# Five small moves in the order of work: P1's copy, the fills beside attention and routing, the keys' sums, a query transpose, and the weighing of kept results

## The chip, the cores and the metric

The kernel runs on one core of a Trainium2 chip. The metric is the time of one execution on the device, in microseconds (us); the profile shows one execution of the same program. Five engines run their own instruction queues in order and meet through semaphores: TensorE (PE), VectorE (DVE), ScalarE (ACT), GpSimd (POOL) and SyncE (SP), which here only issues DMA transfers.

## The reference

All arithmetic is in float32. The first half is an attention with a polynomial sketch in place of a softmax, over 4 batches, 4 heads, 1088 tokens and a head size of 32:

```python
def phi(x):                       # r = 8, so 64 features
    a = np.einsum('rd,bhsd->bhsr', S1, x)
    b = np.einsum('rd,bhsd->bhsr', S2, x)
    return np.einsum('bhsi,bhsj->bhsij', a, b).reshape(*x.shape[:-1], r * r)
kv  = np.einsum('bhsf,bhsd->bhfd', phi(k), v)
z   = np.sum(phi(k), axis=2)
num = np.einsum('bhsf,bhfd->bhsd', phi(q), kv)
den = np.einsum('bhsf,bhf->bhs', phi(q), z)[..., None] + 1e-06
attn = num / den
```

Its output, as 4352 tokens of 128 values, is the input x of the second half, eight experts with Sinkhorn weights:

```python
P = np.exp(x @ w_gate - (x @ w_gate).max())
for _ in range(8):
    P /= P.sum(1, keepdims=True) + 1e-09
    P /= P.sum(0, keepdims=True) + 1e-09
    P *= N / E
for e in range(E):                # w1[e]: 128 x 1024, w2[e]: 1024 x 128
    out += P[:, e:e + 1] * (np.maximum(x @ w1[e], 0.0) @ w2[e])
```

## The kernel before

**Two streams in one order.** The experts' work is by far the larger part. It is a generator, `steps` (from L1124), that yields after each small step: one `first` product (x times w1, L929, followed by the relu on ScalarE, L933) and the `second` products (h times w2, L1114) that are due then, `LAG` = 8 steps after the block that they belong to began. `fill(n)` (L1189) draws steps from it until n shares are used up; a step of 480 columns is one share, so that a step of 256 columns is 0.53 and one of 416 is 0.87. Attention and routing are written around it: they issue some instructions, and then `fill` or a `yield` puts expert work behind them on the queues. A larger number at such a place means that more expert work stands ahead of what comes next. The order on TensorE and DVE is kept as written (`manual_schedule`); ScalarE, GpSimd and SyncE follow a scheduler once the start is over, except where `keep_in_program_order` stands.

**Experts ahead of routing.** Before the routing weights are known, the kernel computes some expert results without weights and keeps them in SBUF (`kept`): all tokens for expert 0, and tokens 0 to 511 and 512 to 1279 for expert 1. These are the groups ahead of `PLAIN`. The other groups scale x by the weight first (`prepare_x`, which writes `xe` on GpSimd), and `weigh_kept` multiplies the kept results by their weights on GpSimd, from `pb`, a broadcast load of the weights. It does so once in each weighted group, and what it gives is added to the sums later.

**Products by sums.** The second products use schemes with fewer multiplications (seven products for 2 x 2 blocks, twenty for 3 x 4 blocks). DVE makes the sums of hidden blocks that they need (L946 for seven, L993 and L1013 for twenty), and the products accumulate in four PSUM banks `s`, which the next group uses again. When a bank of a group is complete, `part` takes it apart. In `part_of_seven` bank 0 holds P1; ScalarE copies its two halves crosswise to `z`, DVE adds P1 itself to z (L756), and P1 stays in the bank (`own["p1"] = s`) until bank 1 has been copied to `m`: then `add_now(y1[lower], own["p1"][lower], m[lower])` is queued on DVE, behind whatever was recorded before.

**Attention.** Batch 0 has a path of its own at the start. For batches 1 to 3, `attention(b)` sums over the keys (`keys_sums`, L352, into a PSUM bank), copies that to `kvs` (`keys_kept`, L368 on DVE and L370 on ScalarE), multiplies the query factors in three parts (`times`, L468, where `rb` arrives by DMA), forms the numerators (`tops`, L477 and L481), divides (`over`), and sends the result through DRAM to `xT` (`take_over`). Between these the next batch's keys and queries are prepared, among them `transpose_q(3)` and `keys_products`.

**Routing.** `routing` computes logits (L511), and then eight rounds: DVE makes row sums, reciprocals and column sums `cs`; after a yield of 4.5 shares TensorE adds `cs` over the partitions (L621). The weights go to DRAM (`pT`), from where `xe` and `pb` are loaded.

**The end.** `last_part` puts together the last group's output. For k == 2 it ends with a transpose and store of y2 (`put`), and one add that y1's last sum needs.

Of the kernel before, what the change touches and what calls it, by code (L numbers as in the profile page):

```python
# [50 lines left out]
def kernel(  # L51
# [307 lines left out]
    def keys_kept(b):  # L359
        pv = sums_of.pop(b)  # L360
        for s in range(2):
            sl = slice(64 * s, 64 * (s + 1))
            if b:
                x, y = kvs[b % 2][sl, :, s, :], pv[sl].rearrange("p i c d -> p i (c d)")[:, :, 0:D + 1]
            else:
                x, y = kvz[sl, :, :, s, :], pv[sl].rearrange("p i c d -> p c i d")
            if s and b:
                nc.vector.tensor_copy(x, y)  # L368
            else:
                nc.scalar.copy(x, y)  # L370

    chunks = ((0, 512), (512, 800), (800, S))

# [148 lines left out]
    def attention(b):  # L522


        follows = b + 1 < B
        keys_sums(b)
        times(b, 0)
        yield 1.4
        keys_kept(b)
        times(b, 1)  # L530
        tops(b, 0)
        if b == 1:
            transpose_q(2)
        yield 1.4
        times(b, 2)
        over(b, 0)
        tops(b, 1)
        if b == 1:
            queries_ab(2)
            repeat_a(2)  # L540
        if follows:
            repeat_b(b + 1)
        yield 1.4
        over(b, 1)
        if b + 1 == B:
            take_over(b, 0, 192, nc.gpsimd)
        yield 1.4
        tops(b, 2)
        if follows:
            transpose_k(b + 1)  # L550
        if b + 2 < B:
            load_k(b + 2)
            load_v(b + 2)
        yield 1.4
        over(b, 2)
        if b + 1 < B:
            take_over(b, 0, W9, nc.gpsimd)
        else:
            take_over(b, 192, W9, nc.sync)
        if follows:  # L560
            yield 0.7
            keys_ab(b + 1)
            yield 0.7
            keys_products(b + 1, 0)
            if b == 1:
                transpose_q(3)
            yield 1.4
            keys_products(b + 1, 1)
            if b == 1:
                queries_ab(3)  # L570
                repeat_a(3)
            yield 1.4
            keys_products(b + 1, 2)
            yield 1.4
# [11 lines left out]
    def routing():  # L586

        yield 5
        for c in range(len(chunks)):
            logits(c)  # L590
        yield 1
        for c in range(len(chunks)):
            logits_turned()
        lg = lgp[:, :, 0:E]
        mx = sk.tile([P, 1], F32, tag="mx", name="mx")
        nc.vector.tensor_reduce(out=mx, in_=lg, axis=AX.XY, op=Alu.max)
        yield 3
        pm = bank()[:, 0:P]
        for s in range(2):
            nc.tensor.matmul(pm[64 * s:64 * (s + 1)], mx.to_broadcast([P, 64]), ident, start=True, stop=True,  # L600
                             tile_position=(0, 64 * s))
        nc.vector.reduce_max(mx, pm, axis=AX.X)
        nc.vector.tensor_scalar(mx, mx, -1.0, 64 * math.log(2.0), op0=Alu.mult, op1=Alu.add)
        pw = p2s[0]
        nc.scalar.activation(out=pw[:, :, 0:E], in_=lg, func=Act.Exp, bias=mx[:, 0:1])

        step = 1.5 * 2.0 ** (23 - 149 + 64)
        nc.vector.tensor_scalar(pw[:, :, 0:E], pw[:, :, 0:E], step, step, op0=Alu.add, op1=Alu.subtract)
        for it in range(ITERS):
            rs = sk.tile([P, SA], F32, tag="rs", name="rs")  # L610
            nc.vector.reduce_sum(rs, pw, axis=AX.X)
            nc.vector.reciprocal(rs, rs)
            p1 = p1s[it % 2]
            nc.vector.scalar_tensor_tensor(p1[:, 0:SA], rs.unsqueeze(2).to_broadcast([P, SA, E]), UP,
                                           pw[:, :, 0:E], op0=Alu.mult, op1=Alu.mult)
            cs = sk.tile([P, E], F32, tag="cs", name="cs")
            nc.vector.reduce_sum(cs, p1.rearrange("p g e -> p e g"), axis=AX.X)
            yield 4.5
            pc = bank()[:, 0:E]
            for s in range(2):  # L620
                nc.tensor.matmul(pc[64 * s:64 * (s + 1)], ones[:, 0:64], cs, start=True, stop=True,  # L621
                                 tile_position=(0, 64 * s))
            cr = sk.tile([P, E], F32, tag="cr", name="cr")
            nc.vector.reciprocal(cr, pc)
            last = it == ITERS - 1
            pw = lgp if last else p2s[(it + 1) % 2]
            nc.vector.scalar_tensor_tensor(pw[:, :, 0:E], cr.unsqueeze(1).to_broadcast([P, SA, E]),
                                           float(N) / E * (1.0 if last else UP), p1[:, 0:SA],
                                           op0=Alu.mult, op1=Alu.mult)

        nc.vector.transpose(out=lgT.rearrange("p a s -> p (a s)"), in_=lgp.rearrange("p a e -> p (a e)"))
        for b in (1, 0, 2, 3):
            nc.sync.dma_start(out=pT[:, b * S:(b + 1) * S],
                                                  in_=lgT[32 * b:32 * b + E].rearrange("p a s -> p (a s)"))
# [71 lines left out]

    first_weighted = next(j for j, (g, e) in enumerate(items) if g == PLAIN)

    def weigh_kept(g):

        lo, n, t, es, _ = groups[g]
        ys = []
        for e in range(es[0]):
            ys.append(kept[e][:, lo:lo + n * t])
            weigh(ys[e], ys[e], weights_of(e, lo, n * t, "pb"))
        for y in ys[1:]:
            tc.keep_in_program_order(nc.gpsimd.tensor_tensor(ys[0], ys[0], y, op=Alu.add))
        if t == 2:
            k1, k2 = ys[0][upper, 0:n], ys[0][upper, n:2 * n]
            tc.keep_in_program_order(nc.gpsimd.tensor_tensor(k1, k1, k2, op=Alu.subtract))  # L720
# [26 lines left out]
    def part_of_seven(g, k):  # L747

        lo, n, _, es, _ = groups[g]
        s = sums[g][k]  # L750

        def add(out, a, b):
            at_leisure(lambda: nc.vector.tensor_tensor(out, a, b, op=Alu.add))

        def add_now(out, a, b):
            soon.append(lambda: nc.vector.tensor_tensor(out, a, b, op=Alu.add))  # L756

        own = parts.setdefault(g, {})
        y1, y2 = (kept[es[0]][:, lo + t * n:lo + (t + 1) * n] for t in range(2))
        if k == 0:  # L760
            z = own["z"] = room("z", n)
            nc.scalar.copy(z[lower], s[upper])
            nc.scalar.copy(z[upper], s[lower])
            add_now(z, s, z)
            own["p1"] = s
        elif k == 1:
            m = own["m"] = room("m", n)
            nc.scalar.copy(m, s)
            add_now(y1[lower], own["p1"][lower], m[lower])
        elif k == 2:  # L770
            w, f = own["w"], own["f"] = room("w", n), room("f", n)
            nc.scalar.copy(w[lower], s[lower])
            nc.scalar.copy(f[lower], s[upper])
            nc.scalar.copy(f[upper], s[upper])
        else:
            r = room("r", n)
            nc.scalar.copy(r[upper], s[lower])
            own["r"] = r
            own["p7"] = s
        own[k] = True  # L780
        z, w, f, m = (own.get(x) for x in "zwfm")
        if all(own.get(x) for x in (0, 2, 3)) and "v" not in own:
            own["v"] = True
            add_now(w[upper], own["p7"][upper], own["r"][upper])
            add(z, z, w)
            add(y2, z, f)
        if all(own.get(x) for x in range(4)):
            add(y1[upper], z[upper], m[upper])
# [9 lines left out]
    def last_part(g, k):  # L798
# [5 lines left out]
        def add(out, a, b):  # L804
            nc.vector.tensor_tensor(out, a, b, op=Alu.add)
# [10 lines left out]
        elif k == 2:  # L816
            nc.scalar.copy(r[lower], s2[upper])
            nc.scalar.copy(x[lower], s0[lower])
            add(y2[upper], z[upper], s2[upper])
            add(y2[lower], s2[lower], r[lower])  # L820
            put(y2, lo + n, n, (nc.sync, nc.scalar))
            add(x[upper], x[upper], s2[upper])
        else:
            add(y1, s1, x)
            put(y1, lo, n, (nc.sync, nc.scalar))
# [298 lines left out]
    def steps():  # L1124

        todo, sums_at, t = {}, {}, 0
        for k in range(len(blocks) + 5):
# [5 lines left out]
            if k < len(blocks):  # L1133
# [13 lines left out]
                    w = w1, w2, sums_of_two(items[j + 1][1], w2)  # L1147
                    loaded_w.update({i: w for i in loaded_w if items[i][1] == items[j + 1][1]})
                if q == 0:
                    if weighted and e == es[3 if tiles == 3 else 2]:  # L1150
                        weigh_kept(g)
                if k == len(blocks) - HELD:
                    kept_to_sums(g)
                m, step, sums_ = (four if tiles == 3 else two)(k)
# [63 lines left out]
    with tc.manual_schedule(engines={engines.DVE, engines.PE}):  # L1218
# [1 line left out]
            multiply(1, i)  # L1220
        transpose_k(1)
        load_k(2)
        fill(0.75)
        fractions(1, 1)
        fractions(1, 0)
        fill(0.75)
# [61 lines left out]
```

## Time and profile before

| what | value |
|---|---|
| time, median of 3 runs (lowest to highest) | 932.78 us (928.51 to 933.78) |
| span of the profiled execution, granted TensorE clock | 927.0 us, 0.999 |
| DVE busy, 100 to 125, 125 to 150, 150 to 175 us | 18.01, 22.59, 22.03 of 25 |
| ScalarE busy in the same stretches | 12.03, 12.79, 13.09 of 25 |
| GpSimd's wait for `pb` to land | 47.2 us in 5 waits |
| `kept` weighed by GpSimd near 400 us, two multiplies | 4.12 us |

The profile page gives each engine's busy time, its idle time with what ended it, and the chain of work that ended last. An idle stretch of an engine that isn't on that chain costs nothing. The first numerators follow some 34 us after the start, the logits come at 105.6 us, the weights go to DRAM at 174.8, and the first product of a weighted group starts at 191.9; from there to the end the work is regular.

### The profile page before, as it was taken

How to read it: one execution, taken by the hardware profiler on the slowest of the kernel's cores; microseconds unless marked ns; L12 is line 12 of the kernel's file. 1: busy time of each engine (PE TensorE's matmuls, PEld its weight loads, DVE VectorE, ACT ScalarE, POOL GpSimd, SP SyncE). 2: the span in 40 equal slices, each digit the busy share in tenths (PEclk: the TensorE clock that was granted, in tenths of full speed). 3: DMA queues.
4: the chain of work that ended last, by engine and by line, in shares of the span. 5: the costliest groups of instructions: out<-in, count | busy, mean ns of one | idle time of the engine just before them, and what ended most of it. 6: DMA issues, size and time to landing. Idle time of an engine off the chain costs nothing.

```text
span 927.0 us, 18876 instructions
## 1 busy us (share of the span) xinstructions
PE 914.0 (99%) x7466; PEld 552.6 (60%) x7466; DVE 673.4 (73%) x1140; ACT 412.6 (45%) x888; POOL 211.3 (23%) x220
## 2 busy tenths in 40 slices
PE   9999999999999999999999999999999999999997
PEld 6777444456666666655555555555555555556886
DVE  7544688797879697685876666965657977768665
ACT  3333455554444454434544444544445444445443
POOL 3031300093546402030120101101010224320220
PEclk9999999999999999999999999999999999999999
DMA  9994100213354434453444434363434365553640
GB/s 252 310 273 153 52 1 1 76 56 109 125 166 159 154 130 144 133 186 110 148 126 155 147 121 136 114 189 125 148 109 155 101 200 183 172 181 92 173 153 12
DMA packets 91303, 128.13 MB, mean 138 GB/s; under 512 B 25392, under 2 KB 69504, under 8 KB 86480
## 3 DMA queue, kind: packets, MB, share of 16 engines
q1 hardware_dynamic: 88384, 121.42, 41.7%
q0 software_dynamic: 1600, 5.36, 2.0%
q8 instruction: 58, 0.95, 0.4%
q10 hardware_dynamic: 1232, 0.16, 0.1%
q14 instruction: 29, 0.24, 0.1%
HBM read 107.88 MB, written 19.05 MB: 137 GB/s over the span
## 4 chain that ended last, share of the span: by engine, by line
PE 95%; DVE 3%; ACT 1%; issue 1%; POOL 0%; DVEq 0%; ACTq 0%; POOLq 0%
PE a L929 49%; PE s L1114 42%; PE a L352 1%; PE a L477 1%; PE a L114 1%; DVE hb L993 1%; PE a L319 0%; DVE pqg L993 0%; PE s L384 0%; PE a L441 0%; ACT hb L933 0%; PE s L407 0%; DVE kept L756 0%; PE a L511 0%; PE a L390 0%
## 5 line engine op out<-in xcount | busy, mean ns | idle before, releaser
L929 PE MATMUL a<-xe,w 128*64 128x256 f32 (+1 forms) x2560 | 519.5, 470 | 0.0
L933 ACT ACTIVATE hb<-a 128x256 f32<-128x256 f32 (+4 forms) x408 | 195.3, 480 | 257.8 <-PE a L929 231.7
L933 ACT ACTIVATE hx<-a 128x256 f32<-128x256 f32 (+1 forms) x360 | 167.4, 465 | 214.2 <-PE a L929 193.8
L929 PEld LDWEIGHTS a<-xe,w 128*64 128x64 f32 x2560 | 208.2, 137 | 77.2 <-issue 1.4
L1114 PE MATMUL s<-hb,ws 128*64 128x256 f32 (+2 forms) x1248 | 214.1, 395 | 0.6 <-DVE hb L993 0.6
L993 DVE TENSOR_TENSOR hx<-hx 128x512 f32<-128x512 f32 (+1 forms) x204 | 157.6, 783 | 68.2 <-ACT hx L933 62.7
L1114 PE MATMUL s<-hx,ws 128*64 128x256 f32 x1280 | 206.0, 379 | 0.7 <-DVE kept L756 0.7
L993 DVE TENSOR_TENSOR hb<-hb 128x512 f32<-128x512 f32 (+1 forms) x204 | 134.5, 670 | 92.2 <-ACT hb L933 88.0
L693 POOL TENSOR_TENSOR xe<-xT,xe 128x768 f32<-128x768 f32 (+2 forms) x41 | 83.3, 2032 | 499.3 <-DMA xe<-pT 485.0
L1114 PEld LDWEIGHTS s<-hx,ws 128*64 128x64 f32 x1280 | 106.7, 137 | 97.4 <-issue 74.0
L1114 PEld LDWEIGHTS s<-hb,ws 128*64 128x64 f32 x1248 | 101.9, 137 | 103.4 <-issue 80.0
L1114 PE MATMUL s<-hb,w 128*64 128x256 f32 (+3 forms) x616 | 116.5, 406 | 2.7 <-DVE kept L756 2.7
L929 PE MATMUL a<-xT,w 128*64 128x416 f32 (+3 forms) x512 | 117.3, 462 | 0.1
L1114 PEld LDWEIGHTS s<-hb,w 128*64 128x64 f32 x616 | 54.0, 137 | 35.6 <-issue 15.2
L1114 PE MATMUL s<-hx,w 128*64 128x256 f32 x384 | 68.5, 379 | 0.0
L929 PEld LDWEIGHTS a<-xT,w 128*64 128x64 f32 x512 | 47.0, 137 | 28.4 <-issue 21.5
L242 POOL TENSOR_TENSOR ws<-w 128x256 f32<-128x256 f32 (+1 forms) x70 | 60.1, 894 | 14.7 <-DMA w<-in_moe_w_dram 10.6
L946 DVE TENSOR_TENSOR hb<-hb 128x416 f32<-128x416 f32 (+3 forms) x60 | 46.4, 774 | 18.7 <-ACT hb L933 10.4
L946 DVE TENSOR_TENSOR hx<-hx 128x256 f32<-128x256 f32 (+1 forms) x65 | 39.1, 607 | 24.4 <-ACT hx L933 23.2
L993 DVE TENSOR_TENSOR pqg<-hb 128x512 f32<-128x512 f32 x68 | 44.5, 696 | 0.0
L1114 PEld LDWEIGHTS s<-hx,w 128*64 128x64 f32 x384 | 34.4, 137 | 10.3
L993 DVE TENSOR_TENSOR pqg<-hx 128x512 f32<-128x512 f32 x68 | 37.4, 591 | 0.0
(183 smaller groups left out, 466.6 us busy)
## 6 DMA issues: line engine op xcount, KB each, us to landing
w<-in_moe_w_dram SPq DMA_DIRECT2D x82, 512.0 KB, 5.3
ws<-ws SPq DMA_DIRECT2D x34, 1024.0 KB, 5.0
xe<-pT SPq DMA_DIRECT2D x34, 384.0 KB, 4.1
ws<-ws SPq DMA_DIRECT2D x12, 512.0 KB, 4.7
ph<-qa SPq DMA_DIRECT2D x12, 288.0 KB, 5.4
rb<-qb SPq DMA_DIRECT2D x3, 1152.0 KB, 7.9
pb<-pT SPq DMA_DIRECT2D x6, 384.0 KB, 7.5
kx<-in_k_dram SPq DMA_DIRECT2D x4, 544.0 KB, 4.9
```

The lines of the kernel that those rows point to most:

```text
L114: nc.tensor.matmul(warm[:, 0:P], ones, ones, start=True, stop=True)
L242: tc.keep_in_program_order(nc.gpsimd.tensor_tensor(ws[:, c:c + len(ns)], blocks(x), blocks(y), op=Alu.subtract if off else Alu.add))
L352: nc.tensor.matmul(pv[64 * s:64 * (s + 1), i], kp[0:n, H * t + h].rearrange("p i j -> p (i j)"), vx[0:n, slots[h], t, :], start=(t == 0 an ...
L477: nc.tensor.matmul(pn[64 * s:64 * (s + 1), t, 2 * i:2 * i + 2].rearrange("p h d -> p (h d)"), ph[:, i, s, 64 * t:64 * (t + 1)], kvs[b % 2] ...
L693: tc.keep_in_program_order(nc.gpsimd.tensor_tensor(out, x, pb, op=Alu.mult))
L929: nc.tensor.matmul(ph[sl], loaded_w[j][0][:, P * f + H2 * s:P * f + H2 * (s + 1)], sources[j][:, lo:hi], start=True, stop=True, tile_posit ...
L933: nc.scalar.activation(out=out, in_=ph, func=Act.Relu)
L946: nc.vector.tensor_tensor(out, a, b, op=Alu.subtract)
L993: nc.vector.tensor_tensor(out if not isinstance(out, tuple) else places(*out), places(*a), places(*b) if isinstance(b, tuple) else b, op=A ...
L1114: nc.tensor.matmul(sums[g][i][H2 * s:H2 * (s + 1), n * place:n * (place + 1)], w, x, start=c == 1, stop=c == per, tile_position=(0, H2 * s))
```

## The change

The edits are:

- `keys_kept`: both halves of the keys' sums are copied by ScalarE; one was DVE's.
- `attention`: more expert work between the keys' sums and the first numerators (2.2 shares for batch 1, 1.7 for batches 2 and 3, from 1.4), so that TensorE has work while the numerators' inputs get ready. `transpose_q(3)` comes ahead of the first keys' product.
- At the start, `fill(1.25)` in place of 0.75 ahead of batch 0's second fractions.
- `routing`: 4.25 shares per round in place of 4.5.
- `weigh_kept`: one multiply for each expert of the group, from its second on, in place of all in one go at the fourth (third in the last group).
- `part_of_seven`: the lower half of P1 is copied out of PSUM by ScalarE, to a buffer `x`, and the later add reads the copy.
- `last_part`: y1's add is put ahead of y2's transpose and store.

```diff
@@ -364,10 +364,7 @@
                 x, y = kvs[b % 2][sl, :, s, :], pv[sl].rearrange("p i c d -> p i (c d)")[:, :, 0:D + 1]
             else:
                 x, y = kvz[sl, :, :, s, :], pv[sl].rearrange("p i c d -> p c i d")
-            if s and b:
-                nc.vector.tensor_copy(x, y)
-            else:
-                nc.scalar.copy(x, y)
+            nc.scalar.copy(x, y)
 
     chunks = ((0, 512), (512, 800), (800, S))
 
@@ -525,7 +522,7 @@
         follows = b + 1 < B
         keys_sums(b)
         times(b, 0)
-        yield 1.4
+        yield 2.2 if b == 1 else 1.7
         keys_kept(b)
         times(b, 1)
         tops(b, 0)
@@ -561,9 +558,9 @@
             yield 0.7
             keys_ab(b + 1)
             yield 0.7
-            keys_products(b + 1, 0)
             if b == 1:
                 transpose_q(3)
+            keys_products(b + 1, 0)
             yield 1.4
             keys_products(b + 1, 1)
             if b == 1:
@@ -615,7 +612,7 @@
                                            pw[:, :, 0:E], op0=Alu.mult, op1=Alu.mult)
             cs = sk.tile([P, E], F32, tag="cs", name="cs")
             nc.vector.reduce_sum(cs, p1.rearrange("p g e -> p e g"), axis=AX.X)
-            yield 4.5
+            yield 4.25
             pc = bank()[:, 0:E]
             for s in range(2):
                 nc.tensor.matmul(pc[64 * s:64 * (s + 1)], ones[:, 0:64], cs, start=True, stop=True,
@@ -706,13 +703,13 @@
 
     first_weighted = next(j for j, (g, e) in enumerate(items) if g == PLAIN)
 
-    def weigh_kept(g):
+    def weigh_kept(g, i):
 
         lo, n, t, es, _ = groups[g]
-        ys = []
-        for e in range(es[0]):
-            ys.append(kept[e][:, lo:lo + n * t])
-            weigh(ys[e], ys[e], weights_of(e, lo, n * t, "pb"))
+        ys = [kept[e][:, lo:lo + n * t] for e in range(es[0])]
+        if i < len(ys):
+            weigh(ys[i], ys[i], weights_of(i, lo, n * t, "pb"))
+            return
         for y in ys[1:]:
             tc.keep_in_program_order(nc.gpsimd.tensor_tensor(ys[0], ys[0], y, op=Alu.add))
         if t == 2:
@@ -761,8 +758,9 @@
             z = own["z"] = room("z", n)
             nc.scalar.copy(z[lower], s[upper])
             nc.scalar.copy(z[upper], s[lower])
+            own["p1"] = room("x", n)
+            nc.scalar.copy(own["p1"][lower], s[lower])
             add_now(z, s, z)
-            own["p1"] = s
         elif k == 1:
             m = own["m"] = room("m", n)
             nc.scalar.copy(m, s)
@@ -818,8 +816,8 @@
             nc.scalar.copy(x[lower], s0[lower])
             add(y2[upper], z[upper], s2[upper])
             add(y2[lower], s2[lower], r[lower])
+            add(x[upper], x[upper], s2[upper])
             put(y2, lo + n, n, (nc.sync, nc.scalar))
-            add(x[upper], x[upper], s2[upper])
         else:
             add(y1, s1, x)
             put(y1, lo, n, (nc.sync, nc.scalar))
@@ -1147,8 +1145,8 @@
                     w = w1, w2, sums_of_two(items[j + 1][1], w2)
                     loaded_w.update({i: w for i in loaded_w if items[i][1] == items[j + 1][1]})
                 if q == 0:
-                    if weighted and e == es[3 if tiles == 3 else 2]:
-                        weigh_kept(g)
+                    if weighted and 1 <= es.index(e) <= es[0] + 1:
+                        weigh_kept(g, es.index(e) - 1)
                 if k == len(blocks) - HELD:
                     kept_to_sums(g)
                 m, step, sums_ = (four if tiles == 3 else two)(k)
@@ -1220,7 +1218,7 @@
             multiply(1, i)
         transpose_k(1)
         load_k(2)
-        fill(0.75)
+        fill(1.25)
         fractions(1, 1)
         fractions(1, 0)
         fill(0.75)
```

## The prediction, made before the changed kernel ran

> **What bounds the kernel now.** I read the page's first block, then TensorE's waits, then the timeline around each wait.
>
> ```profile
> PE 914.0 (99%) x7466; PEld 552.6 (60%) x7466; DVE 673.4 (73%) x1140; ACT 412.6 (45%) x888; POOL 211.3 (23%) x220
> PE 95%; DVE 3%; ACT 1%; issue 1%; POOL 0%; DVEq 0%; ACTq 0%; POOLq 0%
> ...
> PE s L1114 <- DVE kept L756: 3.5, 4, 1.2
> PE a L477 <- ACT hb L933: 1.4, 2, 0.9
> ...
> PE s L1114 <- DVE hb L993: 0.6, 1, 0.6
> PE s L407 <- DVE ph L399: 0.4, 1, 0.4
> PE a L441 <- DVE qT L302: 0.3, 1, 0.3
> ```
>
> The first two lines are the page's busy shares and its chain; the rest are TensorE's waits (us, times, longest). TensorE is the chain. Of 927.0 us it is idle for 13: 1.0 before its first matmul, 5.0 after its last (output stores), 6.93 in twelve gaps between. No matmul is removed by the diff, so only those gaps, and what is hidden beside them, can be won. Hidden: a 128x256 record lasts 379 ns but pairs start 0.213 apart, so a drained array loses 0.17 us more than the gap shown. At 119.03 the pair before started at 117.27 and the pitch is 0.35, so the loss is 1.41 us for a gap of 1.19; at 34.48 it is 1.08 for 0.91.
>
> The timelines of three of these gaps (start, us, engine, what; in brackets the idle time and its releaser):
>
> ```profile
> 114.46 0.59 DVE L756 TENSOR_TENSOR z<-s,z 128x416 f32<-128x416 f32 x1
> ...
> 118.40 0.57 DVE L756 TENSOR_TENSOR kept<-s,m 64x416 f32<-64x416 f32 x1
> ...
> 119.03 0.56 PE L1114 MATMUL s<-hb,w 128*64 128x416 f32 x1 [1.19 <-DVE kept L756]
> ...
> 33.16 0.96 DVE L468 TENSOR_TENSOR ph<-ph,rb 128x768 f32<-128x768 f32 x1 [4.68 <-DMA rb<-qb]
> ...
> 34.15 0.23 DVE L368 COPY kvs<-a 64x66 f32<-64x66 f32 x1
> ...
> 34.48 0.92 PE L477 MATMUL a<-kvs,ph 128*64 128x66 f32 x24 [0.91 <-ACT hb L933]
> ...
> 400.28 4.12 POOL L693 TENSOR_TENSOR kept<-kept,pb 128x768 f32<-128x768 f32 x2 [12.25 <-DMA pb<-pT]
> ...
> 404.60 2.30 DVE L993 TENSOR_TENSOR hb<-hb,pqg 128x512 f32<-128x512 f32 x1
> ...
> 409.18 0.65 PE L1114 MATMUL s<-hb,ws 128*64 128x256 f32 x4 [0.55 <-DVE hb L993]
> ```
>
> First: the last reader of the old P1 in PSUM is a DVE add 3.9 us behind the add of z that also reads it; five routing instructions stand between. Second: the page names ScalarE, but its hb had long ended; what ended last is DVE's copy of the second kvs half, queued behind a multiply that waited for a DMA. Third: three GpSimd instructions and an xe in a row (400.28 to 408.58) stretch DVE's sums.
>
> **What the Trainium skill says.** "PSUM — Partial Sum Buffer", section "PSUM bank collisions raise a hardware error", wants PSUM guarded by bank and quadrant: the next group's first product waits for every reader of the bank, as at 119.03. "SBUF — State Buffer", "Who interferes with whom", says that a DVE instruction with two SBUF inputs contends with a GpSimd one that reads SBUF. The trace agrees: the same 128x512 subtraction on hb took 0.69 us at 399.81 with GpSimd idle, and the add at 404.60 took 2.30 under it. "Perfetto Trace Analysis", "Optimizing Scalar/DVE Operations", advises moving work to ScalarE when DVE is saturated: in 125 to 175 us DVE is busy 44.6 of 50, ScalarE 25.9.
>
> **P1 copied out** (part_of_seven). Adds five ScalarE copies of 64 partitions: the neighbouring z copies took 0.50 us at 416 columns (three) and 0.48 at 384 (two), 2.5 us in all. Behind each are queued the copy of m and the next relu; a relu there started 0.2 us after its matmul ended (117.78, 117.97), and each of the four banks gives one step of 1.4 us, so 0.5 is hidden. DVE does as many adds as before. The bank is now free after the add of z. In the first group that is 115.05 (the copy itself about 114.9), 2.5 us before TensorE would arrive at 117.61. In the second and third the old add of z ended at 140.75 and 162.68, which would still be late for an arrival near 140.4 and 162.2, but the built order puts this add ahead of the round's DVE chain, which took 2.76 us there (136.36 to 139.12), and its inputs were there (ScalarE's second z copy ended at 137.29 and 159.29). The fourth wait, 0.72 at 203.37, had its z done at 200.35. All four go: 3.45 of gaps plus 4 x 0.17 = **4.1 us**.
>
> **Attention: more work ahead, ScalarE copies, transpose sooner.** The built order says how many steps (0.86 us at 256 columns, 1.4 at 416) stand ahead of each point. Before the second fractions one step more (0.43, no second product yet): the multiply they wait for ends 0.39 after arrival, so that gap goes. Before batch 1's numerators two steps more: arrival 33.40 - 0.56 + 1.72 = 34.56, after the multiply's end at 34.12 (rb landed at 33.04, from issues that don't move), and kvs, two ScalarE copies of 0.21, is ready by 31.5. Gap gone, 0.4 spare. Batch 2's gets three more, one of them after keys_sums; its waits were 0.08 and 0.06. Batch 3's gap of 0.48 was DVE's copy, 87.40 to 87.63 behind an hb sum of 1.02; ScalarE can do it from 85.1, and the multiply, though now behind that sum, has the sum's inputs two steps earlier: gap gone. queries_ab(3) waited 0.31 for a transpose that took 1.23 behind a product of 1.23: with the order swapped it goes, and the keys' sums behind, at 57.5, have over 4 us. Sum 0.39 + 0.91 + 0.14 + 0.48 + 0.31 = 2.23, plus 6 x 0.17: **3.2 us**.
>
> **Routing closer.** Yields of 4.25: eight quarters give back what the fills added (0.5 + 0.8 + 2 x 0.3 = 1.9), and in the built order the last rounds stand at the same place. Nothing is won by itself. Spare: the first cs ended at 118.48, TensorE's use came at 122.57; the closest round loses one step, 1.4, of 4.1. **0.**
>
> **weigh_kept spread out.** At most one product (2.06) and one xe (2.27) now adjoin, 4.3 us where 8.3 did; the single stall of 0.55 + 0.17 goes: **0.7 us**. In the first weighted group it moves up two experts: xe then ends at 242.6 + 2.3 = 244.9 at worst, and its expert starts near 248.8 (18.95 us each from 191.9). Hidden.
>
> **Tail swap.** The last add of y1 stands behind both swapped instructions (0.42 and 0.45) either way. **0.**
>
> Sum 4.1 + 3.2 + 0.7 = 8.0. New waits: DVE's 44.6 us in that stretch now face about 48, 93%. I put one wait of the smallest present size (0.70 + 0.17) there and 0.6 at the logits, where batch 3's last transfer landed at 104.48 and TensorE came at 105.57. The unknown is bounded by nothing and by all of the P1 gain, 4.1; I take 1.5. Net **-6.5**: 932.78 - 6.5 = **926.3 us**.
>
> **Rivals.** (B) The stalls move rather than go: DVE at 93% delays hb sums as it delayed the kept adds, and TensorE waits there. For it: DVE's share. Against it: the sums have some three steps, 4 us, before their products. Then the P1 gain returns and 1.4 more at logits and numerators: 8.0 - 4.1 - 1.4 = 2.5, **930.3**. (C) Slower: work ahead pushes the batches back against their DMA chain, batch 3's into other traffic. Its xd and xT took from 98.1 to 104.48; batch 1's, beside loads, took 46.26 to 62.86, 10.2 longer. With 1.1 spare that is a stall of 9.1; with 3 more from B's waits, 932.78 - 8.0 + 9.1 + 3.1 = **937**. Against it: the stretch before the logits keeps its seven steps, and batch 1's xT has 16 us spare (landed 62.86, used 78.93).
>
> **How the numbers follow.** Chances: mine 0.66, B 0.22, C 0.12. A change over 0.5% is 4.7 us, so faster begins below 928.1. The three times of before spread over 5.3 us, and mine clears the bound by 1.8 only: of 0.66, 0.58 are faster and 0.08 same; of B 0.04, 0.17 and 0.01 slower; of C 0.01 same, 0.11 slower. Faster 0.62, same 0.26, slower 0.12. The low end is all 8.0 gained and a fast run (the fastest before was 4.3 under its median), taken half: 922; the high end holds B with a slow one, 931.5; C is left out.
>
> **What would show it.** Right: no wait of L1114 on kept's P1 add; no gap over 0.1 before the three numerators; DVE sums under 2 us near 400; TensorE's inner gaps near 1.5 instead of 6.9, with 0.63 left before the first fractions at 13.64, which nothing touches. Wrong: new TensorE waits on hb sums or cs in 100 to 200 us, a wait before the logits, or a first xe product that comes late.

## The result, and the profile after

The changed kernel takes 922.64 us (median of six runs, 922.40 to 924.09), the kernel before 929.75 beside it (six, 928.51 to 933.78). The ratio is 0.9917, with a 95% interval of 0.9895 to 0.9939: 7.1 us less. The prediction had 6.5 us less than 932.78; 922.6 lies near the low end of its range, because 932.78, a median of three, was 3.0 us above the median of six. The two profiled executions took 928.73 us before and 922.97 after, with spans of 927.0 and 921.1 us.

These are the lines of the page after, busy shares and chain, and then all of TensorE's waits in it (us, times, longest):

```profile
PE 911.2 (99%) x7466; PEld 740.6 (80%) x7466; DVE 665.8 (72%) x1137; ACT 413.3 (45%) x896; POOL 213.4 (23%) x220
PE 98%; DVE 1%; DMA 1%; ACT 0%; issue 0%; SPq 0%; DVEq 0%
...
PE s L1112 <- DVE w L753: 1.5, 1, 1.5
PE a L319 <- DVE kT L307: 1.1, 1, 1.1
PE a L114 <- POOL own L116: 1.0, 1, 1.0
PE a L404 <- ACT kvz L367: 0.6, 1, 0.6
PE a L478 <- issue: 0.6, 1, 0.6
```

TensorE has as many matmuls as before. The list of waits is what changed: the four on the P1 add, those before the numerators, the fractions and the query transpose, and the one at 409 us are gone. The gaps within its work sum to 3.8 us where they were 6.9. Three are new. The wait for kT comes at the start, where the warm-up matmuls (L114) ended sooner; its L319 starts at 7.13 us, before at 7.22, so it costs nothing. The 0.57 at an eps matmul (66.17 us) is in this profile alone, not in that of a second run of the same kernel, and stays unexplained. The wait on the "w" add, P7's, comes again in that second profile (1.49).

With the prediction's hidden 0.17 us per gap the sum comes out for these two profiles: the eleven gaps closed are 6.23 + 1.87 = 8.1 us, the two that cost something take 1.48 + 0.57 + 0.34 = 2.4, which leaves 5.7 of the 5.9 us between the two spans. For the other ten profiles the same sum is off by 0.2 to 0.9 us, and once by 1.7, so it is good to about 1 us, and the 0.17 by itself is not confirmed. The medians differ by 1.2 us more than the spans, since the execution profiled before was 1.0 us under the median of its kernel and the one after 0.3 over.

Here is the new wait, from the timelines of DVE, ScalarE and TensorE in the kernel after (start, us, engine, what; in brackets the idle time before and its releaser):

```profile
112.82 0.59 DVE L753 TENSOR_TENSOR z<-s,z 128x416 f32<-128x416 f32 x1 [0.60 <-ACT x L762]
113.62 0.58 DVE L753 TENSOR_TENSOR kept<-x,m 64x416 f32<-64x416 f32 x1 [0.21 <-ACT m L766]
114.99 0.29 DVE L599 TENSOR_REDUCE mx<-a 128x1 f32<-128x128 f32 x1 [0.78 <-PE a L597]
115.31 0.15 DVE L600 TENSOR_SCALAR mx<-mx 128x1 f32<-128x1 f32 x1
...
116.15 0.50 ACT L775 COPY r<-s 64x416 f32<-64x416 f32 x1
116.67 0.52 ACT L602 ACTIVATE p<-kT,mx 128x272 f32<-128x272 f32 x1
...
117.22 0.30 DVE L605 TENSOR_SCALAR p<-p 128x272 f32<-128x272 f32 x1 [1.75 <-ACT p L602]
...
120.57 0.59 DVE L753 TENSOR_TENSOR w<-s,r 64x416 f32<-64x416 f32 x1
...
121.31 0.54 PE L1112 MATMUL s<-hb,ws 128*64 128x416 f32 x1 [1.48 <-DVE w L753]
```

The add of P1 now reads the copy `x` and holds no bank. But routing's first chain (seven DVE instructions, of which the prediction counted the five behind the exponential), which stood between the adds of z and of P1, stands between the adds of P1 and of P7 (`w<-s,r`), and P7's bank is held in its place. DVE also stands idle ahead of that chain, 0.78 us for TensorE's transposed maximum, and inside it, 1.75 us. The exponential's input `mx` is ready at 115.46, but ScalarE starts the exponential at 116.67, behind the copies with which it empties the group's banks.

### The profile page after: what moved, and what is told of

Read it like the earlier page. It is cut to its first block, busy times and chain, and to the rows that moved or that the text cites. A ratio compares the mean times of both kernels' runs of the same rounds, so it can differ in the third digit from the quotient of the medians.

```text
span 921.1 us, 18889 instructions
## 1 busy us (share of the span) xinstructions
PE 911.2 (99%) x7466; PEld 740.6 (80%) x7466; DVE 665.8 (72%) x1137; ACT 413.3 (45%) x896; POOL 213.4 (23%) x220
## 4 chain that ended last, share of the span: by engine, by line
PE 98%; DVE 1%; DMA 1%; ACT 0%; issue 0%; SPq 0%; DVEq 0%
PE a L927 51%; PE s L1112 43%; PE a L352 1%; PE a L474 1%; DMA kx<-in_k_dram 1%; PE a L319 0%; PE s L381 0%; PE a L438 0%; PE s L404 0%; PE a L508 0%; PE a L387 0%; PE a L404 0%; PE a L618 0%; DVE hb L944 0%; DVE y L803 0%
## 5 line engine op out<-in xcount | busy, mean ns | idle before, releaser
L927 PE MATMUL a<-xe,w 128*64 128x256 f32 (+1 forms) x2560 | 596.1, 470 | 0.0
L927 PEld LDWEIGHTS a<-xe,w 128*64 128x64 f32 x2560 | 303.7, 137 | 20.7
L1112 PE MATMUL s<-hb,ws 128*64 128x256 f32 (+2 forms) x1248 | 249.6, 395 | 1.5 <-DVE w L753 1.5
L1112 PE MATMUL s<-hx,ws 128*64 128x256 f32 x1280 | 239.4, 379 | 0.0
L1112 PEld LDWEIGHTS s<-hb,ws 128*64 128x64 f32 x1248 | 156.9, 137 | 55.8 <-issue 4.6
L1112 PEld LDWEIGHTS s<-hx,ws 128*64 128x64 f32 x1280 | 160.9, 137 | 47.3
L1112 PE MATMUL s<-hb,w 128*64 128x256 f32 (+3 forms) x616 | 126.7, 406 | 0.0
L1112 PEld LDWEIGHTS s<-hb,w 128*64 128x64 f32 x616 | 67.6, 137 | 18.0 <-issue 6.0
L1112 PE MATMUL s<-hx,w 128*64 128x256 f32 x384 | 78.2, 379 | 0.0
L242 POOL TENSOR_TENSOR ws<-w 128x256 f32<-128x256 f32 (+1 forms) x70 | 61.9, 918 | 11.4 <-DMA w<-in_moe_w_dram 11.1
L1112 PEld LDWEIGHTS s<-hx,w 128*64 128x64 f32 x384 | 46.3, 137 | 2.7
```

Source lines behind the costliest of these rows:

```text
L242: tc.keep_in_program_order(nc.gpsimd.tensor_tensor(ws[:, c:c + len(ns)], blocks(x), blocks(y), op=Alu.subtract if off else Alu.add))
L927: nc.tensor.matmul(ph[sl], loaded_w[j][0][:, P * f + H2 * s:P * f + H2 * (s + 1)], sources[j][:, lo:hi], start=True, stop=True, tile_posit ...
L1112: nc.tensor.matmul(sums[g][i][H2 * s:H2 * (s + 1), n * place:n * (place + 1)], w, x, start=c == 1, stop=c == per, tile_position=(0, H2 * s))
```

## The experiments

Line numbers shift a little from edit to edit. The kernel before, timed beside the others in five rounds, had medians of 928.78 us (first four rows), 929.19 (next four) and 929.52 (last two).

| kernel | median us (lowest to highest) | ratio to before (95%) |
|---|---|---|
| after, P1 left in PSUM | 925.20 (924.76 to 926.90) | 0.9969 (0.9956 to 0.9981) |
| before, P1 copied | 925.35 (924.51 to 926.88) | 0.9966 (0.9953 to 0.9978) |
| after, weighed at once | 922.49 (922.37 to 924.18) | 0.9939 (0.9926 to 0.9953) |
| after, attention and routing as before | 925.78 (924.39 to 928.02) | 0.9970 (0.9960 to 0.9980) |
| after, amounts of work as before | 923.29 (921.59 to 926.39) | 0.9947 (0.9931 to 0.9963) |
| after, half of the keys' sums by DVE | 922.82 (922.62 to 922.94) | 0.9936 (0.9924 to 0.9948) |
| after, P7 copied too | 922.72 (922.50 to 924.29) | 0.9940 (0.9927 to 0.9953) |
| before, weighing spread | 928.19 (926.68 to 931.76) | 0.9995 (0.9985 to 1.0005) |
| after, maximum sooner | 920.38 (919.86 to 921.07) | 0.9899 (0.9881 to 0.9916) |
| after, again | 922.48 (921.37 to 924.39) | 0.9923 (0.9905 to 0.9940) |

### P1, undone and alone

Undone in the kernel after:

```diff
-            own["p1"] = room("x", n)
-            nc.scalar.copy(own["p1"][lower], s[lower])
             add_now(z, s, z)
+            own["p1"] = s
```

> The changed kernel with P1 left in PSUM as before; all else as changed. Theory A (each part closes its own TensorE waits, and the parts add up): the waits of the second products on the DVE add of P1 come back at three or four places, 0.7 to 1.2 us each, and the new wait on the P7 add at 121 us (1.48 us) goes, since TensorE is held by the P1 add before it. Net 1.5 to 2.6 us longer than the changed kernel's 922.6: 924.1 to 925.2. Theory B (the gain is the attention's and routing's new places, which alone move DVE's routing chain away from the P1 adds): no wait on the P1 add, 922.6.

It took 925.20, 2.6 us more than the changed kernel: theory A, in the time. TensorE's waits:

```profile
PE s L1111 <- DVE kept L753: 2.6, 3, 1.1
PE s L1111 <- DVE w L753: 1.5, 1, 1.5
```

Three P1 waits return, in the second, third and fourth groups. In the first none does, since the P1 add (112.16) is already ahead of routing's chain (from 113.90), as in the changed kernel. And the P7 wait stays, at 1.48: what was expected of it was wrong, and it isn't P1's copy that makes it.

The same edit the other way round, in the kernel before:

> The kernel before with P1 copied out of PSUM and nothing else. Theory A: its four waits on the P1 add go (3.45 us of gaps and 0.17 hidden beside each, 4.1), and one wait on another add may come in the first group, 1.5: 2.6 to 4.1 us less than the kernel before, 925.7 to 927.2 for a kernel before of 929.8. Theory B: the same time as before, since the P7 and hb adds stand behind the same DVE chain and TensorE waits for them in its place.

925.35, 3.4 us less than the kernel before beside it: theory A, within its 2.6 to 4.1 us. Its profile has no wait on the P1 add and none on P7's, but two that are left on the add of z, which still reads the bank (with the one near 405 us that this kernel kept):

```profile
PE s L1115 <- DVE hb L994: 0.6, 1, 0.6
PE s L1115 <- DVE z L756: 0.5, 2, 0.3
```

This is what the prediction worked out for the second and third group: the copy alone brings the bank's release to the end of z's add, which TensorE waits for by 0.19 and 0.35 us there, and it takes the other order of DVE's queue, which the attention's and routing's moves bring, to close them.

### The weighing, undone and alone

```diff
-                    if weighted and 1 <= es.index(e) <= es[0] + 1:
-                        weigh_kept(g, es.index(e) - 1)
+                    if weighted and e == es[3 if tiles == 3 else 2]:
+                        weigh_kept(g)
...
```

> The changed kernel with the kept results weighed in one go as before. Theory A: one TensorE wait of about 0.55 us on a DVE sum returns near 400 us, with 0.17 hidden, and DVE's sums there take over 2 us where they take 0.7: 0.7 us longer, 923.3. Theory B: the old wait hung on the place of the other work at that moment and doesn't return: 922.6.

922.49, as the changed kernel: theory B, in the time. The timeline near 400 us (GpSimd and DVE):

```profile
396.00 4.14 POOL L690 TENSOR_TENSOR kept<-kept,pb 128x768 f32<-128x768 f32 x2 [13.04 <-DMA pb<-pT]
396.15 4.54 DVE L991 TENSOR_TENSOR hb<-hb 128x512 f32<-128x512 f32 x2
400.22 2.15 POOL L714 TENSOR_TENSOR kept<-kept,kept 128x768 f32<-128x768 f32 x1
...
400.72 1.93 DVE L1011 TENSOR_TENSOR hb<-pqg,hb 128x256 f32<-128x256 f32 x1
...
402.33 2.00 POOL L690 TENSOR_TENSOR xe<-xT,xe 128x768 f32<-128x768 f32 x1
```

GpSimd's run of four is back, and two DVE sums take 4.54 us where a like pair on hx took 1.48 without it, at 406.58 us in the changed kernel. So GpSimd does lengthen DVE's sums. They don't run beside it at a lower rate, though: a lengthened sum ends a fixed time after the GpSimd instruction beside it. The one of 256 columns here ends at 402.65, 0.28 us after GpSimd's 402.37. Of the 102 lengthened sums from 190 us on in the kernel before, all but one end 0.28 to 0.29 us (256 columns) or 0.54 to 0.55 us (512) after GpSimd. That is less than these sums take alone (0.42 and 0.69), so it seems that DVE stands until GpSimd has finished, and four GpSimd instructions in a row let four sums through. Not every sum that begins beside GpSimd is held: 9 of 52 that begin well before its end take their usual time.

But here the run begins after the block's pair of pqg sums (ended at 395.63), and no TensorE wait follows; the only one on a DVE sum is 0.21 us at 876.8. In the kernel before, it began at 400.28, 0.14 us ahead of that pair. When it begins is set by the landing of `pb`, on which GpSimd waits. In the two profiles that have the old weighing in the old order of work, before and P1 alone, the wait is there in both (0.55 and 0.58).

> The kernel before with the weighing of kept results spread over several experts and nothing else. Theory A (the sum of TensorE waits): the 0.55 us wait near 405 to 409 goes, 0.7 us less than the kernel before. Theory B (as undoing it in the changed kernel gave nothing, whether GpSimd's run of four meets DVE's sums at a bad moment is chance of where the pb transfer lands): DVE's sums there still shorten from over 2 us to about 0.7 to 1.2, but the time is within 0.3 us of before.

928.19, with an interval of the ratio that holds 1. The wait of 0.55 us is gone from its profile, but the time can't tell 0.7 from nothing: its single times spread over 5.1 us, and its profile holds a wait of 2.12 us elsewhere, before batch 1's numerators. By the waits, the weighing is worth 0.7 us where GpSimd's run meets the block's sums badly, and nothing where it doesn't.

### The attention's and routing's part, whole and split

Undone: the yields of 1.4 and 4.5, the fill of 0.75, DVE's copy, and the late transpose.

> The changed kernel with the attention's and routing's part undone (yields of 1.4 and 4.5, first fill of 0.75, half of the keys' sums copied by DVE, batch 3's queries transposed after the first product); P1 copied and weighing spread. Theory A: the waits before the numerators and fractions return, 2.23 us of gaps and 0.17 beside each of six: 3.2 us longer than the changed kernel, 925.8; and the wait on the P7 add changes its size. Theory B: about 926 to 929, since these moves are all of the gain but the weighing's 0.7.

925.78, 3.1 us more than the changed kernel: as theory A says, though theory B's range begins close by, at 926; what speaks against B is the gain of P1 alone. The P7 wait is gone, not only of another size. The execution profiled was the slowest of eight, 928.02, and shows more than the predicted waits, in lines of TensorE's:

```profile
PE a L477 <- issue: 3.1, 1, 3.1
...
PE s L1115 <- DVE z L756: 0.5, 2, 0.3
PE a L477 <- ACT hb L934: 0.5, 1, 0.5
PE s L407 <- DVE ph L399: 0.4, 1, 0.4
PE a L441 <- DVE qT L302: 0.3, 1, 0.3
```

The 3.1 us stand before batch 2's numerators. The page says "issue", but DVE's timeline shows what was missing:

```profile
62.57 0.96 DVE L468 TENSOR_TENSOR ph<-ph,rb 128x768 f32<-128x768 f32 x1 [11.15 <-DMA v<-in_v_dram]
63.56 0.23 DVE L368 COPY kvs<-a 64x66 f32<-64x66 f32 x1
...
63.89 0.92 PE L477 MATMUL a<-kvs,ph 128*64 128x66 f32 x24 [3.12 <-issue]
```

The first multiply by `rb` waited for a transfer (the profile names a load of v that came last; in the second run of the changed kernel it names rb for the same wait), the copy followed, and TensorE came last. In the profile of the kernel before the same multiply began at 57.57, 5.0 us sooner, with rb issued at the same time (49.34 in both) and the same instructions ahead of it. So how long the transfers there take differs between executions. That the change covers this at batch 2 is not shown: in the second run of the changed kernel the multiply began at 62.36, and the numerators waited 1.78 us. Of the twelve profiles, one of the five without the new amounts of work waits there, and one of the seven with them. From the issue of rb to where TensorE comes to these numerators there are 12.8 us in the kernel before and 11.4 here, but only 11.0 and 10.7 in the two profiles of the changed kernel, which issues rb later.

At batch 1 it is shown. There TensorE comes to the numerators 7.9 to 8.9 us after the issue of rb in the five profiles without the amounts, and 9.1 to 9.7 us after it in the seven with them. The five wait 0.91, 1.14, 0, 1.01 and 2.12 us, longest where rb landed last (33.66) and not at all where it landed first (31.70); none of the seven waits more than 0.11. So this wait, too, differs between executions, and the 0.91 of the one profile was not its size in every run.

Only the amounts of work put back:

```diff
-        yield 2.2 if b == 1 else 1.7
+        yield 1.4
...
-            yield 4.25
+            yield 4.5
...
-        fill(1.25)
+        fill(0.75)
```

> The changed kernel with the amounts of expert work as before (first fill 0.75, attention's yields 1.4, routing's 4.5); keys' sums still copied by ScalarE, batch 3's queries still transposed sooner. Theory A (the fills are what covers the late rb transfers and the fractions, and they also put routing's first DVE chain ahead of the P7 add): the 0.39 wait on the fractions returns, batch 1's numerators wait about 0.6 us for the multiply and batch 2's up to 3 us when rb lands late, but the 1.48 us wait on the P7 add goes: 923 to 925, and the single times spread more (over 2 us). Theory B (the ScalarE copies are what helps, and the fills nothing): 921 to 922.5, with the P7 wait gone and no wait at the numerators.

923.29, and single times that spread over 4.8 us: theory A. Its profiled execution took 921.59, faster than any of the changed kernel's first six, although three waits returned:

```profile
PE a L474 <- ACT hb L931: 1.0, 1, 1.0
...
PE s L1112 <- DVE z L753: 0.6, 2, 0.4
PE s L404 <- DVE ph L396: 0.4, 1, 0.4
```

Those on z's add, as with P1's copy alone, show that it was the amounts that brought DVE's other order. The P7 wait is not among them. By these waits the amounts close 1.96 us of gaps, with 0.17 beside each of four, and open 1.48 with 0.17, in the first routing chain, 1.0 in all; the medians differ by 0.65. The wait for the query transpose is not among them either: the transpose, still sooner here, closes it by itself. Undoing the whole part cost 2.5 us more than this; the waits of 0.48 and 0.31 that the copies and the transpose close, with 0.17 beside each, are 1.1 of it, and the rest is open.

> The changed kernel with one half of the keys' sums copied by DVE as before. Theory A (fills matter): the copy stands behind the rb multiply and, for batch 3, an hb sum of 1.0 us, but TensorE comes up to two steps later than before, so at most 0.3 us at one numerator: 922.6 to 923.2. Theory B (the ScalarE copies matter): waits of 0.5 to 0.9 at batches 1 and 3 return, 923.8 to 924.5.

The edit restores the branch `if s and b: nc.vector.tensor_copy(x, y)`. 922.82, the changed kernel's time, and no wait above 0.06 us at a numerator: with the fills in place the copies by ScalarE are worth nothing that can be measured. Without the fills the copies close batch 3's 0.48, which the kernel with the amounts as before doesn't show. Either of the two suffices there. At batch 1 the fills do it: this kernel has no wait there, the one before it 1.01.

### The new wait

```diff
             own["r"] = r
-            own["p7"] = s
+            own["p7"] = own["p1"]
+            nc.scalar.copy(own["p7"][upper], s[upper])
```

> The changed kernel with the upper half of P7 copied out of PSUM by ScalarE as well (into the unused half of P1's copy), so that no DVE add of the seven products holds bank 3 into the next group. Theory A (the bank held by the P7 add behind routing's first chain is the whole of the 1.48 us wait at 121 us): the wait goes, with 0.17 beside it, and five more ScalarE copies of 0.5 us are hidden: 1.6 us less than the changed kernel, 921.0. Theory B (DVE is simply too late there): TensorE waits for the hb sums, which stand behind the same add, in its place, and the time stays 922.6.

922.72: theory B. The bank is free, and TensorE waits at the same place for the next thing in DVE's queue:

```profile
116.85 0.30 DVE L605 TENSOR_SCALAR p<-p 128x272 f32<-128x272 f32 x1 [2.27 <-ACT p L602]
...
120.81 1.22 DVE L945 TENSOR_TENSOR hb<-hb 128x416 f32<-128x416 f32 x2
...
121.45 0.56 PE L1113 MATMUL s<-hb,ws 128*64 128x416 f32 x1 [1.13 <-DVE hb L945]
```

And the extra ScalarE copy, ahead of the exponential, made DVE's standstill longer, 2.27 for 1.75, so 0.52 of the 1.13 may be the copy's own doing. The bank was the form of the wait; behind it DVE is late, with the sums behind it, for it stands still for the maximum and for an exponential that ScalarE has queued behind the copies of the group's end. This suggests an edit that moves the maximum, and with it the exponential and the chain:

```diff
-        yield 3
+        yield 1.25
...
-            yield 4.25
+            yield 6.0 if it == 0 else 4.25
```

> The changed kernel with 1.75 shares of the work moved from ahead of routing's maximum over the partitions to ahead of the first round's sums (yield 3 becomes 1.25, the first 4.25 becomes 6.0), so that the exponential stands on ScalarE after the copy of m, as in the kernel before, and not behind all the first group's copies; the fills of the attention stay as changed. Theory A (the wait at 121 us is DVE's queue standing still for an exponential that ScalarE has queued behind nine instructions of the group's end): DVE's idle time before the exponential's user falls from 1.75 us to about 0.6, the 1.48 us wait goes, none takes its place: 1.6 us less than the changed kernel, 921.0. Theory B (DVE is too full there in any order): the wait moves to an hb sum or to the second group, as it did when P7 was copied out, and the time stays within 0.3 of the changed kernel's.

> The changed kernel once more, beside the one with the maximum sooner, so that the two are timed on the same chip in the same rounds. All theories: 922.4 to 924.1 as in its six earlier runs, with the 1.48 us wait on the P7 add in its profile.

920.38 against 922.48 in the same rounds, with ranges that don't touch: 2.1 us less than the changed kernel, and 9.1 less than before. Theory A, and 0.5 us more than its 1.6. DVE's timeline in this kernel:

```profile
111.69 0.59 DVE L753 TENSOR_TENSOR z<-s,z 128x416 f32<-128x416 f32 x1 [0.60 <-ACT x L762]
112.20 0.28 DVE L599 TENSOR_REDUCE mx<-a 128x1 f32<-128x128 f32 x1
...
113.26 0.30 DVE L605 TENSOR_SCALAR p<-p 128x272 f32<-128x272 f32 x1 [0.59 <-ACT p L602]
...
117.10 0.59 DVE L753 TENSOR_TENSOR w<-s,r 64x416 f32<-64x416 f32 x1
```

And all of TensorE's waits in it:

```profile
PE a L114 <- POOL own L116: 1.0, 1, 1.0
PE a L404 <- ACT kvz L367: 0.6, 1, 0.6
```

The standstill for the exponential is down to 0.59 us from 1.75 and that for the maximum to nothing from 0.78, so P7's add follows z's by 5.41 us where it was 7.75. The two went together, and no run tells them apart: the chain is back between the adds of z and P1. Between the first matmul and the last one gap is left, the 0.63 that no edit touches. It is the best of the versions run.

## Why the prediction was right, and where its terms were off

**What bounds the kernel.** Right. TensorE's gaps, with 0.17 beside each, account for the difference of the spans to within 0.2 us. With all but one closed in the last experiment the span is 918.1, 8.8 less than before, where the sum gives 8.1.

**P1, 4.1 us.** The mechanism held. Alone the copy gave 3.4 and its removal cost 2.6, since in the first group the new order closes that wait as well. The term was too large by these 0.7 to 1.5.

**Attention, 3.2 us.** Undoing it cost 3.1, but that is what is left after the P7 wait that the same moves make (1.48 and 0.17), so what they close is worth more than the 3.2, about 4.8 by this sum. The prediction didn't weigh two parts of it: the waits on z's add in the second and third group, which come back without the moves, and rb's landing, by which batch 1's wait alone differs from 0 to 2.12 us between executions. At batch 3 the prediction put the gain down to ScalarE's copies; there the fills alone do it too.

**Routing, 0.** The closer rounds kept their slack: no TensorE wait on cs is in the profile. But the step that costed this part at nothing looked only at the rounds. It missed the first chain, ahead of them: the fills of the attention move the maximum two steps back (288 first products stand ahead of it in TensorE's order where there were 280, four to a step), across the end of a group, and the exponential lands behind that group's copies on ScalarE.

**Weighing, 0.7.** Not to be had in the changed kernel: undone, it gave 922.49 for 922.64. That GpSimd lengthens DVE's sums was right and was seen again, but whether TensorE waits for it depends on when the run begins, which the other moves changed. That the xe of the first weighted group stays hidden was right.

**New waits, 1.5.** Near: 1.48 and 0.17. The prediction placed it in that stretch by DVE's 93%, and in part at the logits. DVE was indeed busy for 47.1 of the 50 us from 125 to 175, and no wait came there. The one wait came ahead of it, from DVE's idle time, and none at the logits. So the size was close by luck, and its reason was not right.

**Tail, 0.** From the last matmul to the end it was 5.02 us before and 5.03 after. This swap wasn't timed alone.

**The sum.** 6.5 for 7.1 is closer than its terms: P1 and the weighing were taken too large, the attention too small. The gaps within TensorE's work did not fall to the 1.5 us that was named as a sign, but to 3.8, of which 1.11 cost nothing.

**The rivals.** (B), that the stalls move, happened for one of eleven. (C), batches late against their DMA chain, didn't: no wait before the logits is in any profile. The transfer that is late at times is rb; the change covers that at batch 1, and is not shown to at batch 2.

## What to carry to other kernels

Where one engine is the bound and 99% busy, list its gaps with the instruction that ended each, and ask what stands ahead of that instruction on its own queue: freeing the buffer that the wait named left 1.13 of the 1.48 us, and moving the instructions for which the queue stood still left nothing. Amounts of covering work do two things, they fill a gap and they move what is behind them across other work, so after such a change look for what it pushed over a group's end. A wait for a DMA that is absent in one profile can be 1.78 us in the next one of the same kernel, so a gap behind a transfer should be read from more than one profile.

## What the runs showed that was not expected

The rb transfer of batch 2, issued at 49.34 us in two kernels that are the same up to there, was followed by DVE's multiply at 57.57 in one and at 62.57 in the other. A wait that the page gives to "issue" was four times (1.14 and 2.12 us at batch 1, 3.12 and 1.78 at batch 2) one for DVE's multiply after such a transfer. And a DVE sum that GpSimd lengthens ends 0.55 us after GpSimd's instruction at 512 columns and 0.28 at 256, not a multiple of its own time later.
